# Scores in four quadrants of TensorE and two PSUM banks, in one visit with the preceding pair's values

## The chip, the core and the metric

The kernel runs on one core of a Trainium2 chip. The metric is the device time of one execution in microseconds (us); the number given for a kernel is the median of several executions. A profiled execution leaves a trace with the start and length of each instruction. Its engines are named PE (TensorE's matmuls), PEld (TensorE's loads of weights), DVE (VectorE), ACT (ScalarE), POOL (GpSimd) and SP (SyncE, which issues the DMAs here).

## The reference

A chunked local attention is followed by two feed-forward layers:

```python
# q, k, v: (4, 8, 768, 64); mem_k, mem_v: (4, 8, 8, 64)
for c in range(24):                       # chunks of 32 queries
    k_full = concat(mem_k, k[c*32-16 : c*32+32+8])   # cut at the ends of the sequence
    scores = q_c @ k_full.T / 8
    a = exp(scores - max); a = a / (sum(a) + 1e-9)
    out_c = a @ v_full
x = out as (3072 tokens, 512)
h = x @ w_in;  g = max(0.01*h, h);              y = g @ w_out     # d_ff 2048
h = y @ w_in2; g = h * clip(h + 3, 0, 6) / 6;   result = g @ w_out2
```

## The kernel before

**Attention.** A "pair" is 64 tokens, two chunks of 32, with all eight heads, taken as HP = 4 pairs of heads; the 4 x 768 tokens make 48 pairs. A pair's context has W = 96 columns: 64 tokens, 16 left, 8 right, 8 of memory; a table of masks takes out what a chunk must not see. The steps of a pair are one function each: `load_qk` and `load_v` (SP), `a_scores` (PE, L317: eight float32 matmuls of 64x64x96, the two heads of a pair of heads on the tiles (0,0) and (64,64) of the array, all into one PSUM bank), `a_masked` (DVE, L327: scale, mask and copy to SBUF), `a_most` (DVE, L339: maximum), `a_exp` (ACT, L346, four activations that also sum), `a_sums` (DVE, L357, L358), `a_norm` (POOL, L362), the transposition of the weights, `a_values` (PE, L394: eight float32 matmuls, 96 rows by 64 columns, on the tiles (0,0) and (0,64)), and `a_xh` (ACT, L406) with `a_xl` (DVE, L412), which split the result into a high and a low part for the feed-forward matmuls. The transposition is made by PE and ACT for the first 16 pairs (`a_turn_pe` L380, `a_turned` L385), by 12 DVE stream transposes a pair after that (`a_turn` L372).

**Feed-forward.** Each layer goes over six blocks of TB = 512 tokens, each block over NF = 16 steps of 128 hidden columns. A step has 24 matmuls of 128x128x512 (`mm3`, L458; three products of high and low parts, high*high, high*low and low*high, stand for one of higher precision): 12 for the hidden columns into a bank `ph`, then, a step later, 12 for the four output parts into the four banks `py0` to `py3`, in which a block's 16 steps are summed. So a block has 384 of them. Between the two, ACT and DVE apply the activation and split (`act_1` to `act_4`: L477, L491, L500, whose result `gl` the last matmuls read). At a block's end `done` copies the four banks, `py0` and `py2` by DVE (L532), `py1` and `py3` by ACT (L534), and `stored` (L543) sends them out. Weights come as 64-bit numbers and are turned into a high and a low part by ACT and DVE (`w_upper` to `w_low`, L217 to L257), during block 0 for layer 1 of the model (called layer 0 in the code) and during block 5 for the other.

**Order.** All steps are put into one `Program` with an engine, an assumed time (the table `TIME`), a due time, the steps they come after, and the buffers they take and free (`rings`: PSUM has four banks `py`, two `ph`, two `pa`). `Program.order` then lists them: each engine always takes the ready step that is due first and for whose buffers there is room, and the code is emitted in that order. Pairs 0 to 7 run in a prologue (TensorE has `keep_warm` matmuls, L551, as long as it has nothing else before the assumed time BEGIN = 30), pairs 8b to 8b + 7 among the feed-forward matmuls of block b - 1. A pair's scores and its values are two steps with due times 7 apart (times `spread`), each in a `pa` bank of its own, so each interrupts the feed-forward matmuls by itself. The prologue's scores and values use the `py` banks.

Of the kernel before, what the change touches and what calls it, by code (L numbers as in the profile page):

```python
# [23 lines left out]
    scores=0.9, masked=0.56, most=0.55, exp=1.65, sums=0.36, norm=0.83, turn=0.6, turned=0.57, turn4=0.95,  # L24
    values=0.6, xh=0.4, xl=0.45, half=1.36, act=0.58, six=0.69, gh=0.6, gl=0.69, done=0.66, warm=0.22,
# [10 lines left out]
class Program:  # L36
# [15 lines left out]
    def order(self, filler):  # L52
# [81 lines left out]
def tile_kernel(  # L134
# [34 lines left out]
    P = 128  # L169
# [23 lines left out]
    masks = at.tile([P, 3, W], F32, tag="masks", name="masks")  # L193
# [6 lines left out]
    rings = dict(w=NF, raw=NRAW, wa=2, ye=4, aT=2, gh=2, gl=2, x=2, py=4, ph=2, pa=2, qk=NBUF, v=NBUF, yn=1, oo=NRAW)  # L200
# [81 lines left out]
    e_t, s_t, m_t, aT_t, px_t, x_t, in_t = {}, {}, {}, {}, {}, {}, {}  # L282
# [24 lines left out]
    def pa(pr, name, early="py"):  # L307
        tag = early if pr < NPB else "pa"
        return ps.tile([P, 512], F32, tag=tag, name=name, bufs=4 if tag == "py" else 2)

    def a_scores(pr):
        qt, kt, _ = inputs(pr)
        pt = pa(pr, f"psc{pr}")
# [7 lines left out]
        e_t[pr] = pt  # L321

    def a_masked(pr):
        p, pt = pr % PPB, e_t[pr]
        mv = 1 if p == 0 else 2 if p == PPB - 1 else 0
        e = sb.tile([P, HP, W], F32, tag="ye", name=f"e{pr}", bufs=4)
        nc.vector.scalar_tensor_tensor(  # L327
            out=e,
            in0=pt[:, :HP * W].rearrange("p (h w) -> p h w", h=HP),
            scalar=SCALE,  # L330
            in1=masks[:, mv:mv + 1, :].to_broadcast([P, HP, W]),
            op0=ALU.mult,
            op1=ALU.add,
        )
        e_t[pr] = e
# [40 lines left out]
    def a_turn_pe(pr):  # L376
        e = e_t.pop(pr)
        pt = pa(pr, f"pt{pr}", "pa")
        for hp in range(HP):
            nc.tensor.transpose(pt[:W, hp * P:(hp + 1) * P], e[:, hp, :], ident)  # L380
        aT_t[pr] = pt

    def a_turned(pr):
        t = at.tile([W, HP, P], F32, tag="aT", name=f"aT{pr}", bufs=2)
        nc.scalar.copy(out=t.rearrange("p h c -> p (h c)"), in_=aT_t[pr][:W, :])  # L385
        aT_t[pr] = t

    def a_values(pr):
        t, vt = aT_t.pop(pr), inputs(pr)[2]
        pt = pa(pr, f"px{pr}")  # L390
# [7 lines left out]
        px_t[pr] = pt[:, :HP * PT].rearrange("p (h c) -> p h c", h=HP)  # L398
# [15 lines left out]
    x_ready, values_done = {}, []  # L414

    def attention(pr, t, turned_by_pe, spread):
# [11 lines left out]
        vl = add("SP", 0.45, due(-1), load_v, pr, takes=vv if blk else (), after=[] if blk else [a], nbytes=W * 2048)  # L428
        s, e, x = [(tag, ("s", pr))], [("ye", ("e", pr))], [("x", (0, blk))]
        before = [values_done[x] for x in [pr - (3 if blk == 0 else 2)] if x >= 0]  # L430
        c = add("PE", T["scores"], due(0), a_scores, pr, after=[a] + before, takes=s, frees=qk if blk else ())
# [14 lines left out]
        p = [(tag, ("v", pr))]  # L446
        c = add("PE", T["values"], due(7.0), a_values, pr, after=[c, vl], takes=p, frees=aT + vv)
        values_done.append(c)
        first = pr % NPB == 0
        c = add("ACT", T["xh"], due(7.8), a_xh, pr, after=[c] + ([] if first else x_ready[blk][:1]),  # L450
                takes=x if first else ())
        d = add("DVE", T["xl"], due(8.3), a_xl, pr, after=[c], frees=p)
        x_ready.setdefault(blk, []).extend([c, d] if first else [d])
# [53 lines left out]
    def output(layer, blk, f, part):  # L507
# [3 lines left out]
        if f == 0 and part == 0:  # L511
            acc[layer, blk] = [
                ps.tile([P, 512], F32, tag="py", name=f"py{layer}_{blk}_{c}", bufs=4) for c in range(4)
            ]
        dst = acc[layer, blk]
# [29 lines left out]
    def keep_warm():  # L545

        if "warm" not in late:
            late["warm"] = ps.tile([P, TB], F32, tag="ph", name="warm", bufs=2)
        for c in range(2):
            r = slice(c * 256, c * 256 + 256)  # L550
            nc.tensor.matmul(late["warm"][:, r], idle[:, :P], idle, start=True, stop=True)  # L551
# [22 lines left out]
    def start():  # L574
# [3 lines left out]
        for e in range(2):  # L578
# [4 lines left out]
            nc.vector.memset(masks[r0, 1, 0:LC], NEG)  # L583
            nc.vector.memset(masks[r1, 2, CTX - RC:CTX], NEG)
# [13 lines left out]
    for pr in range(NP):  # L598
# [3 lines left out]
        else:  # L602
            every = NF * length[0, blk - 1] / NPB
            spread = 1.6 if blk == 1 else 1.5
# [125 lines left out]
```

## Time and profile before

| | us |
|---|---|
| median of 3 runs | 1170.42 |
| lowest and highest | 1169.61, 1171.92 |
| the profiled execution | 1171.43 |
| its span, first to last instruction | 1169.7 |
| PE, DVE, ACT, POOL busy | 1160.6, 601.4, 471.2, 40.5 |
| prologue, before the first feed-forward matmul | 35.23 |
| blocks 0 / 1 to 3, each / 4 / 5 of the first layer | 112.71 / 102.20 / 101.15 / 87.04 |

TensorE's granted clock is 1.00 of full speed in all slices of the page. A matmul's start is exact, its end is modelled, and neighbours overlap: the step from one start to the next is what it costs. A float32 matmul on a part of the array leaves two records ("x16" for eight matmuls).

### The profile page before, as it was taken

What the parts mean: (1) busy time and instruction counts of PE and PEld (TensorE: products, weight loads), DVE (VectorE), ACT (ScalarE), POOL (GpSimd) and SP (SyncE); (2) the same over time, 40 slices, a digit from 0 to 9 for tenths busy, and PEclk for the clock granted to TensorE, in tenths of its full rate; (3) what the DMA queues carried; (4) which work ended last, traced back from release to release, by engine and by line L of the source; (5) the groups of instructions that cost most, each with busy time, mean ns of one, the idle gap of its engine ahead of it and who ended that gap; (6) DMA issues with size and microseconds to landing.
All of it is one profiled execution on the core that took longest, in us unless ns stands there. A gap on an engine that the chain in (4) does not pass through costs nothing.

```text
span 1169.7 us, 16189 instructions
## 1 busy us (share of the span) xinstructions
PE 1160.6 (99%) x6338; PEld 936.1 (80%) x6338; DVE 601.4 (51%) x1291; ACT 471.2 (40%) x1073; POOL 40.5 (3%) x54
## 2 busy tenths in 40 slices
PE   9999999999999999999999999999999999999998
PEld 7777777777777777777888888888888888888886
DVE  5999975555555556554698943323223223222222
ACT  6878842333334333332677633223223223222222
POOL 1100000000000000000000000000000000000000
PEclk9999999999999999999999999999999999999999
DMA  8455521121112112111553500100100100000000
GB/s 240 157 186 181 184 94 37 42 85 37 37 47 81 37 43 84 37 37 35 171 163 126 185 32 4 69 1 13 60 1 22 51 1 5 33 1 14 24 1 36
DMA packets 38572, 78.64 MB, mean 67 GB/s; under 512 B 4192, under 2 KB 16480, under 8 KB 38496
## 3 DMA queue, kind: packets, MB, share of 16 engines
q1 hardware_dynamic: 38496, 77.61, 20.9%
q8 instruction: 50, 0.82, 0.3%
q14 instruction: 26, 0.21, 0.1%
HBM read 65.01 MB, written 12.58 MB: 66 GB/s over the span
## 4 chain that ended last, share of the span: by engine, by line
PE 91%; DVE 5%; DMA 2%; issue 1%; ACT 1%; SPq 0%; DVEq 0%; ACTq 0%
PE py L458 42%; PE ph L458 42%; PE psc L317 3%; PE px L394 2%; DMA raw<-in_moe_w_out_dram 2%; PE warm L551 1%; DVE w L257 1%; DVE wa L238 1%; DVE raw L245 1%; DVE wa L227 1%; DVE wa L231 1%; PE pt L380 0%; DVE gl L500 0%; ACT wa L217 0%; DVE e L327 0%
## 5 line engine op out<-in xcount | busy, mean ns | idle before, releaser
L458 PE MATMUL ph<-xh,w 128*128 128x512 f32 x768 | 259.2, 398 | 1.8 <-ACT w L251 1.0
L458 PE MATMUL ph<-yh,w 128*128 128x512 f32 x768 | 252.0, 389 | 0.0
L458 PE MATMUL py<-gh,w 128*128 128x512 f32 x768 | 243.3, 396 | 0.9 <-DVE w L257 0.5
L458 PE MATMUL py<-w,gh 128*128 128x512 f32 x768 | 236.4, 389 | 0.0
L486 DVE SCALAR_TENSOR_TENSOR ph<-g,ph 128x512 f32<-128x512 f32 x96 | 66.8, 696 | 281.5 <-ACT g L480 281.4
L480 ACT ACTIVATE g<-ph,three 128x512 f32<-128x512 f32 x96 | 66.3, 690 | 294.5 <-PE ph L458 294.5
L458 PEld LDWEIGHTS ph<-xh,w 128*128 128x128 f32 x768 | 143.3, 188 | 38.3 <-DVE w L257 4.0
L458 PEld LDWEIGHTS ph<-yh,w 128*128 128x128 f32 x768 | 144.2, 188 | 30.0
L458 PEld LDWEIGHTS py<-gh,w 128*128 128x128 f32 x768 | 141.0, 188 | 33.9 <-DVE w L257 3.8
L458 PEld LDWEIGHTS py<-w,gh 128*128 128x128 f32 x768 | 144.2, 188 | 29.9
L458 PE MATMUL ph<-xl,w 128*128 128x512 f32 x384 | 149.8, 390 | 0.4 <-DVE xl L412 0.4
L458 PE MATMUL py<-gl,w 128*128 128x512 f32 x384 | 150.0, 390 | 0.0
L458 PE MATMUL py<-w,gl 128*128 128x512 f32 x384 | 149.4, 389 | 0.0
L458 PE MATMUL ph<-yl,w 128*128 128x512 f32 x384 | 149.4, 389 | 0.0
L477 ACT ACTIVATE ph<-ph 128x512 f32<-128x512 f32 x96 | 55.9, 582 | 161.9 <-PE ph L458 161.8
L372 DVE STREAM_TRANSPOSE aT<-e 32x128 f32<-32x128 f32 x384 | 115.7, 301 | 8.4 <-POOL e L362 3.1
L346 ACT ACTIVATE e<-e,mx 128x96 f32<-128x96 f32 x192 | 69.6, 365 | 100.3 <-DVE mx L339 95.8
L500 DVE TENSOR_TENSOR gl<-ph,gh 128x512 fp32r<-128x512 f32 x96 | 66.2, 690 | 73.1 <-ACT gh L491 72.8
L502 DVE SCALAR_TENSOR_TENSOR gl<-ph,gh 128x512 fp32r<-128x512 f32 x96 | 66.3, 691 | 55.6 <-ACT gh L493 55.6
L458 PEld LDWEIGHTS py<-gl,w 128*128 128x128 f32 x384 | 72.1, 188 | 15.0
L458 PEld LDWEIGHTS py<-w,gl 128*128 128x128 f32 x384 | 72.0, 188 | 15.0
L458 PEld LDWEIGHTS ph<-yl,w 128*128 128x128 f32 x384 | 72.0, 188 | 14.9
(52 smaller groups left out, 942.6 us busy)
## 6 DMA issues: line engine op xcount, KB each, us to landing
raw<-in_moe_w_in_dram SPq DMA_DIRECT2D x32, 512.0 KB, 3.6
raw<-in_moe_w_out_dram SPq DMA_DIRECT2D x32, 512.0 KB, 3.6
k<-in_k_dram SPq DMA_DIRECT2D x40, 192.0 KB, 2.6
v<-in_v_dram SPq DMA_DIRECT2D x40, 192.0 KB, 2.5
y_dram<-yo SPq DMA_DIRECT2D x24, 256.0 KB, 2.5
yn<-y_dram SPq DMA_DIRECT2D x6, 1024.0 KB, 5.2
out_dram<-oo SPq DMA_DIRECT2D x24, 256.0 KB, 2.1
q<-in_q_dram SPq DMA_DIRECT2D x40, 128.0 KB, 2.0
```

The costliest lines, as they stand in the source:

```text
L227: nc.vector.tensor_scalar(out=a, in0=a, scalar1=LEAST, scalar2=MOST, op0=ALU.max, op1=ALU.min)
L231: nc.vector.tensor_scalar(out=a, in0=a, scalar1=3, scalar2=0x3FFFFFF8, op0=ALU.logical_shift_left, op1=ALU.bitwise_and)
L317: nc.tensor.matmul(pt[e * PT:(e + 1) * PT, hp * W:(hp + 1) * W], qt[r, hp, :], kt[r, hp, :], start=True, stop=True, tile_position=(e * D, ...
L346: nc.scalar.activation(out=e[:, hp, :], in_=e[:, hp, :], func=AF.Exp, bias=mx[:, hp:hp + 1], accum_out=su[:, hp:hp + 1],)
L372: nc.vector.transpose(out=t[c, :, r], in_=e[r, :, c])
L394: nc.tensor.matmul(pt[e * D:(e + 1) * D, hp * PT:(hp + 1) * PT], vt[:, c], t[:, hp, e * PT:(e + 1) * PT], start=True, stop=True, tile_posi ...
L458: nc.tensor.matmul(dst, a, b, start=first and i == 0, stop=last and i == len(terms) - 1)
L477: nc.scalar.activation(out=ph, in_=ph, func=AF.Prelu, alpha=0.01)
L480: nc.scalar.activation(out=g, in_=ph, func=AF.Relu, bias=three, scale=1.0)
L486: nc.vector.scalar_tensor_tensor(out=ph, in0=g, scalar=6.0, in1=ph, op0=ALU.min, op1=ALU.mult)
L500: nc.vector.tensor_sub(out=gl, in0=ph, in1=gh.bitcast(F32))
L502: nc.vector.scalar_tensor_tensor(out=gl, in0=ph, scalar=1.0 / 6.0, in1=gh.bitcast(F32), op0=ALU.mult, op1=ALU.subtract)
```

## The change

From pair 8 on, a pair's scores and the values of the pair before are one step on PE, a "visit" (`visit`, `visit_step`), and share one PSUM tile of two banks: scores of head pairs 0 and 1 in columns 0 to 191 of bank 0, those of 2 and 3 in the same columns of bank 1, and the values in columns 192 to 447 of bank 1. There is one such tile (`pa`, one buffer of two banks in place of two of one bank). The eight score matmuls go over all four 64x64 quadrants of the array: head pairs of bank 0 on the diagonal as before, those of bank 1 on (0,64) and (64,0), so that in the order written four in a row are on four quadrants. For the latter the two heads of a pair of heads stand in exchanged partitions, which `a_values` undoes by the columns it reads. The first pairs' scores go to `py`, their values to `ph`, their transposes to the one `pa` tile. The four output banks become two tiles of two banks, `py0` with parts 0 and 1, `py1` with 2 and 3. The mask table keeps the common mask alone; the sequence's first and last pair get two small DVE memsets each. `keep_warm` runs until the last PE transposition of the prologue is evacuated. Due times and assumed times change with it.

```diff
-    scores=0.9, masked=0.56, most=0.55, exp=1.65, sums=0.36, norm=0.83, turn=0.6, turned=0.57, turn4=0.95,
-    values=0.6, xh=0.4, xl=0.45, half=1.36, act=0.58, six=0.69, gh=0.6, gl=0.69, done=0.66, warm=0.22,
+    visit=1.2, scores=0.75, masked=0.56, most=0.55, exp=1.65, sums=0.36, norm=0.83, turn=0.6, turned=0.57, turn4=0.95,
+    values=0.85, xh=0.4, xl=0.45, half=1.36, act=0.58, six=0.69, gh=0.6, gl=0.69, done=0.66, warm=0.22,
...
-                    if e == "PE" and filler and now < filler[2]:
+                    if e == "PE" and end[filler[2]] is None:
...
-    rings = dict(w=NF, raw=NRAW, wa=2, ye=4, aT=2, gh=2, gl=2, x=2, py=4, ph=2, pa=2, qk=NBUF, v=NBUF, yn=1, oo=NRAW)
+    rings = dict(w=NF, raw=NRAW, wa=2, ye=4, aT=2, gh=2, gl=2, x=2, py=2, ph=2, pa=1, pt=1, qk=NBUF, v=NBUF, yn=1, oo=NRAW)
...
     def a_scores(pr):
...
-        for hp in range(HP):
-            for e in range(2):
-                r = slice(e * D, (e + 1) * D)
-                nc.tensor.matmul(
-                    pt[e * PT:(e + 1) * PT, hp * W:(hp + 1) * W], qt[r, hp, :], kt[r, hp, :],
-                    start=True, stop=True, tile_position=(e * D, e * PT),
-                )
+        for m in range(HP // 2):
+            for j in range(2):
+                hp = j * HP // 2 + m
+                for e in range(2):
+                    r, n = slice(e * D, (e + 1) * D), e ^ j
+                    nc.tensor.matmul(
+                        pt[n * PT:(n + 1) * PT, j, m * W:(m + 1) * W], qt[r, hp, :], kt[r, hp, :],
+                        start=True, stop=True, tile_position=(e * D, n * PT),
+                    )
...
     def a_masked(pr):
...
+        for n in range(2):
+            if p == 0:
+                nc.vector.memset(e[n * PT:n * PT + CH, :, 0:LC], NEG)
+            if p == PPB - 1:
+                nc.vector.memset(e[n * PT + CH:(n + 1) * PT, :, CTX - RC:CTX], NEG)
...
     def a_values(pr):
...
-                c = slice(hp * P + e * D, hp * P + (e + 1) * D)
+                c, n = slice(hp * P + e * D, hp * P + (e + 1) * D), e ^ 2 * hp // HP
...
-                    pt[e * D:(e + 1) * D, hp * PT:(hp + 1) * PT], vt[:, c], t[:, hp, e * PT:(e + 1) * PT],
+                    pt[e * D:(e + 1) * D, hp * PT:(hp + 1) * PT], vt[:, c], t[:, hp, n * PT:(n + 1) * PT],
...
+    def visit(pr):
+        if pr < NP:
+            a_scores(pr)
+            pt = p_t[pr]
+        else:
+            pt = pa(f"px{pr}")
+        if pr > NPB:
+            a_values(pr - 1, pt[:, 1, HP // 2 * W:HP // 2 * W + HP * PT])
...
-        c = add("PE", T["scores"], due(0), a_scores, pr, after=[a] + before, takes=s, frees=qk if blk else ())
+        if blk == 0:
+            before = [values_done[x] for x in [pr - 3] if x >= 0]
+            c = add("PE", T["scores"], due(0), a_scores, pr, after=[a] + before, takes=s)
+        else:
+            c = visit_step(pr, t, [a], s, qk)
...
-        c = add("PE", T["values"], due(7.0), a_values, pr, after=[c, vl], takes=p, frees=aT + vv)
+        if blk == 0:
+            p = [("ph", ("v", pr))]
+            c = add("PE", T["values"], due(7.0), a_values_first, pr, after=[c, vl], takes=p, frees=aT + vv)
+            values_done.append(c)
+            finish(pr, c, due(7.0), p)
+        else:
+            pending[:] = [c, vl, aT + vv]
+    def visit_step(pr, t, after=(), takes=(), frees=()):
+        if not pending:
+            return add("PE", T["scores"], t, visit, pr, after=after, takes=takes, frees=frees)
+        p = [*takes] or [("pa", ("s", pr))]
+        c = add("PE", T["visit"], t, visit, pr, after=[*pending[:2], *after], takes=p,
+                frees=pending[2] + [*frees])
+        finish(pr - 1, c, t, p)
+        return c
...
-                ps.tile([P, 512], F32, tag="py", name=f"py{layer}_{blk}_{c}", bufs=4) for c in range(4)
+                ps.tile([P, 2, 512], F32, tag="py", name=f"py{layer}_{blk}_{c}", bufs=2) for c in range(2)
...
-            spread = 1.6 if blk == 1 else 1.5
-            attention(pr, block_at[0, blk] - 9.5 * spread - every * (NPB - 1 - i), blk == 1, spread)
+            attention(pr, block_at[0, blk] - 3.5 - every * (NPB - i), blk == 1, 1.3)
+    visit_step(NP, block_at[0, NB - 1] - 3.5)
```

`finish` adds `a_xh` and `a_xl` of a pair behind the step that made its values, as `attention` did before.

How the rows of an engine move, at three places. First PE at steps 12 to 14 of block 1, before: the values of one pair (`px`, L394) stand between output matmuls, the next pair's scores (`psc`, L317) six matmuls later.

```order
L458 MATMUL py_1_1_1903<-gh_1_12_2491,w_12_1462 128x512 x2
L458 MATMUL py_1_1_1903<-gl_1_12_2499,w_12_1462 128x512
L394 MATMUL px_2536<-aT_2501,v_75 64x64 [waits DMAHW3_49,DVE_49,PE_49]
L394 MATMUL px_2536<-aT_2501,v_75 64x64 [waits DVE_49]
L394 MATMUL px_2536<-aT_2501,v_75 64x64 x6
L458 MATMUL py_1_2_1904<-gh_1_12_2491,w_12_1462 128x512 x2
L458 MATMUL py_1_2_1904<-gl_1_12_2499,w_12_1462 128x512
L458 MATMUL py_1_3_1905<-gh_1_12_2491,w_12_1462 128x512 x2
L458 MATMUL py_1_3_1905<-gl_1_12_2499,w_12_1462 128x512
L317 MATMUL psc_2556<-k_74,q_72 64x96 [waits DMAHW5_49,DMAHW4_49,PE_49]
L317 MATMUL psc_2556<-k_74,q_72 64x96 x7
L458 MATMUL ph_1_14_2565<-xh_768,w_14_1610 128x512
```

After, at the same steps (L329 scores, L410 values):

```order
L512 MATMUL ph_1_13_2497<-xl_742,w_13_1530 128x512
L512 MATMUL ph_1_13_2497<-xh_741,w_13_1530 128x512
L329 MATMUL psc_2515<-k_74,q_72 64x96 [waits DMAHW5_49,DMAHW4_49,PE_49]
L329 MATMUL psc_2515<-k_74,q_72 64x96 x7
L410 MATMUL psc_2515<-aT_2479,v_75 64x64 [waits DMAHW3_49,DVE_49]
L410 MATMUL psc_2515<-aT_2479,v_75 64x64 [waits DVE_49]
L410 MATMUL psc_2515<-aT_2479,v_75 64x64 x6
L512 MATMUL py_1_0_1883<-gh_1_12_2483,w_12_1468 128x512 [waits Activation_49]
L512 MATMUL py_1_0_1883<-gh_1_12_2483,w_12_1468 128x512
```

Scores and values now follow one another with no feed-forward matmul between, into the same tile, at the end of the hidden matmuls. Such a visit stands 31 times in blocks 1 to 4, each 48 feed-forward matmuls behind the one before; a last one has values alone. In block 0 there are eight merged visits, and the PE transposes stand by themselves some 30 feed-forward matmuls behind each; before, block 0 had seven visits of scores, six of them followed directly by transposes of the pair before, and eight of values.

Second DVE at the same place, before:

```order
L500 TENSOR_TENSOR gl_1_13_2545<-ph_1_13_2505,gh_1_13_2534 128x512 [waits PE_49,Activation_49]
L412 TENSOR_TENSOR xl_1914<-px_2536,xh_1913 128x4x64 [waits Activation_49]
L327 SCALAR_TENSOR_TENSOR e_2572<-psc_2556,masks 128x384 [waits PE_49]
L339 TENSOR_REDUCE mx_2576<-e_2572 128x4 [waits DVE_49]
L357 TENSOR_SCALAR su_2578<-su_2578 128x4 [waits Activation_49]
L358 RECIPROCAL su_2578<-su_2578 128x4 [waits DVE_49]
L500 TENSOR_TENSOR gl_1_14_2607<-ph_1_14_2565,gh_1_14_2599 128x512 [waits Activation_49]
```

After:

```order
L338 SCALAR_TENSOR_TENSOR e_2541<-psc_2515,masks 128x384 [waits PE_49]
L351 MEMSET e_2541 32x4x8 [waits DVE_49]
L351 MEMSET e_2541 32x4x8
L431 TENSOR_TENSOR xl_1892<-psc_2515,xh_1891 128x4x64 [waits Activation_49]
L554 TENSOR_TENSOR gl_1_13_2550<-ph_1_13_2497,gh_1_13_2533 128x512
L356 TENSOR_REDUCE mx_2558<-e_2541 128x4 [waits DVE_49]
L374 TENSOR_SCALAR su_2560<-su_2560 128x4 [waits Activation_49]
```

The maximum came directly behind the masked scores; now the low part `xl` of the pair before (which waits for ACT) and a feed-forward `gl` stand between them, and in this pair two memsets.

Third ACT at the end of the program, before:

```order
L480 ACTIVATE g_5_15_9372<-ph_5_15_9353,three 128x512 [waits PE_49]
L493 ACTIVATE gh_5_15_9381<-ph_5_15_9353 128x512 [waits DVE_49]
L534 COPY oo_1_9399<-py_5_1_8925 128x512 [waits DMAHW0_49,PE_49]
L534 COPY oo_3_9406<-py_5_3_8927 128x512 [waits DMAHW4_49,DMAHW2_49,DMAHW7_49,DVE_49,PE_49]
L725 UNCONDITIONAL_BRANCH
```

After:

```order
L534 ACTIVATE g_5_15_9325<-ph_5_15_9306,three 128x512 [waits PE_49]
L547 ACTIVATE gh_5_15_9334<-ph_5_15_9306 128x512 [waits DVE_49]
L589 COPY oo_1_9352<-py_5_0_8879 128x512 [waits DMAHW0_49,DVE_49]
L589 COPY oo_3_9359<-py_5_1_8880 128x512 [waits DMAHW4_49,DMAHW7_49,DMAHW2_49,DVE_49]
L777 UNCONDITIONAL_BRANCH
```

ACT's copies of parts 1 and 3 (`oo_1`, `oo_3`) waited for PE; now they wait for DVE, whose copies of parts 0 and 2 read the same tiles.

## Rows read from the trace of the kernel before

**Rows 1.** The page: busy time and share of each engine.

```profile
PE 1160.6 (99%) x6338; PEld 936.1 (80%) x6338; DVE 601.4 (51%) x1291; ACT 471.2 (40%) x1073; POOL 40.5 (3%) x54
```

**Rows 2.** Busy by stretch (blocks 0, 1, 4, 5): us, engines, PEclk, DMA, GB/s.

```profile
core 0: us, PE busy (x) PEld busy (x) DVE busy (x) ACT busy (x) POOL busy (x), PEclk, DMA share, GB/s
...
35.23:147.94 112.71, 109.24 (x658) 81.71 (x657) 106.13 (x213) 91.58 (x213) 6.64 (x8) 1.00 0.59 184
147.94:250.14 102.20, 102.20 (x641) 80.71 (x640) 60.15 (x161) 36.20 (x109) 6.62 (x8) 1.00 0.18 53
...
454.54:555.69 101.15, 101.15 (x626) 80.10 (x624) 54.46 (x152) 33.52 (x99) 6.62 (x8) 1.00 0.16 48
555.69:642.73 87.04, 87.04 (x386) 72.07 (x385) 71.30 (x127) 61.34 (x106) 0.00 (x0) 1.00 0.47 154
```

**Rows 3.** Timeline, PE, scores in block 1: start, length, engine, operation.

```profile
182.27 0.40 PE L458 MATMUL py<-gl,w 128*128 128x512 f32 x1
...
182.60 0.88 PE L317 MATMUL psc<-k,q 64*64 64x96 f32 x16
183.40 0.50 PE L458 MATMUL ph<-xh,w 128*128 128x512 f32 x1
...
183.74 0.39 PE L458 MATMUL ph<-xl,w 128*128 128x512 f32 x1
```

**Rows 4.** Timeline, PE, values among feed-forward matmuls in block 0.

```profile
45.81 0.39 PE L458 MATMUL ph<-xh,w 128*128 128x512 f32 x1
46.12 0.69 PE L394 MATMUL px<-aT,v 96*64 96x64 f32 x16
46.74 0.50 PE L458 MATMUL ph<-xh,w 128*128 128x512 f32 x1
47.08 0.39 PE L458 MATMUL ph<-xl,w 128*128 128x512 f32 x1
```

**Rows 5.** Timeline, PE, the prologue's end: scores, values, scores.

```profile
33.01 0.88 PE L317 MATMUL psc<-k,q 64*64 64x96 f32 x16
33.81 0.69 PE L394 MATMUL px<-aT,in 96*64 96x64 f32 x16
34.43 0.88 PE L317 MATMUL psc<-k,q 64*64 64x96 f32 x16
```

**Rows 6.** Timeline, PE: window 182.55 to 182.61; four transposes in block 0.

```profile
182.60 0.30 PE L317 MATMUL psc<-k,q 64*64 64x96 f32 x2
...
52.15 0.64 PE L380 MATMUL pt<-ident,e 128*96 128x128 f32 x4 [0.23 <-POOL e L362]
52.55 0.47 PE L458 MATMUL ph<-xh,w 128*128 128x512 f32 x1
```

**Rows 7.** Timeline, DVE, POOL, PE, ACT: one pair behind its scores, block 1.

```profile
183.52 0.56 DVE L327 SCALAR_TENSOR_TENSOR e<-psc,masks 128x384 f32<-128x384 f32 x1 [1.57 <-PE psc L317]
...
184.12 0.55 DVE L339 TENSOR_REDUCE mx<-e 128x4 f32<-128x384 f32 x1
...
186.89 0.83 POOL L362 TENSOR_TENSOR e<-e,su 128x384 f32<-128x384 f32 x1 [11.90 <-DVE su L358]
...
188.32 3.78 DVE L372 STREAM_TRANSPOSE aT<-e 32x128 f32<-32x128 f32 x12
...
193.16 0.69 PE L394 MATMUL px<-aT,v 96*64 96x64 f32 x16
...
193.90 0.37 ACT L406 CAST xh<-px 128x256 fp32r<-128x256 f32 x1 [0.78 <-PE px L394]
```

**Rows 8.** Waits in block 0: for what, total us, times, longest.

```profile
PEld ph L458 <- DVE w L257: 4.0, 10, 0.7
PEld py L458 <- DVE w L257: 3.8, 7, 0.9
```

**Rows 9.** Timeline, the last copies and the last matmul.

```profile
1164.50 0.69 DVE L532 COPY oo<-py 128x512 f32<-128x512 f32 x1 [0.67 <-PE py L458]
...
1164.75 0.39 PE L458 MATMUL py<-w,gl 128*128 128x512 f32 x1
1166.07 0.59 ACT L534 COPY oo<-py 128x512 f32<-128x512 f32 x1 [1.66 <-DMA out_dram<-oo]
```

More of the change, by code (lines that the diff above doesn't have):

```diff
@@ L192, in tile_kernel @@
     ident = at.tile([P, P], F32, tag="ident", name="ident")
-    masks = at.tile([P, 3, W], F32, tag="masks", name="masks")
+    masks = at.tile([P, HP // 2, W], F32, tag="masks", name="masks")
     idle = at.tile([P, 256], BF, tag="idle", name="idle")
@@ L412, in a_xl, with finish @@
         nc.vector.tensor_sub(out=xl[:, :, c], in0=px_t.pop(pr), in1=xh[:, :, c].bitcast(F32))
-    x_ready, values_done = {}, []
+    x_ready, values_done, pending, opened = {}, [], [], []
+    def finish(pr, c, t, p):
+        blk = pr // NPB
+        first = pr % NPB == 0
+        c = add("ACT", T["xh"], t + 0.8, a_xh, pr, after=[c] + ([] if first else x_ready[blk][:1]),
+                takes=[("x", (0, blk))] if first else ())
+        d = add("DVE", T["xl"], t + 1.3, a_xl, pr, after=[c], frees=p)
+        x_ready.setdefault(blk, []).extend([c, d] if first else [d])
+    def visit(pr):
[6 more added lines that the diff above has]
+            a_values(pr - 1, pt[:, 1, HP // 2 * W:HP // 2 * W + HP * PT])
     def attention(pr, t, turned_by_pe, spread):
@@ L445, in attention @@
                         frees=e if i == 3 else ())
-        p = [(tag, ("v", pr))]
-        c = add("PE", T["values"], due(7.0), a_values, pr, after=[c, vl], takes=p, frees=aT + vv)
[L448 to L453, printed above, removed]
+        if blk == 0:
+            p = [("ph", ("v", pr))]
+            c = add("PE", T["values"], due(7.0), a_values_first, pr, after=[c, vl], takes=p, frees=aT + vv)
+            values_done.append(c)
+            finish(pr, c, due(7.0), p)
+        else:
+            pending[:] = [c, vl, aT + vv]
[7 more added lines that the diff above has]
+        return c
     def mm3(dst, terms, first, last):
@@ L511, in output @@
         if f == 0 and part == 0:
-            acc[layer, blk] = [
-                ps.tile([P, 512], F32, tag="py", name=f"py{layer}_{blk}_{c}", bufs=4) for c in range(4)
+            pairs = [
+                ps.tile([P, 2, 512], F32, tag="py", name=f"py{layer}_{blk}_{c}", bufs=2) for c in range(2)
             ]
+            acc[layer, blk] = [pairs[c // 2][:, c % 2, :] for c in range(4)]
         dst = acc[layer, blk]
@@ L545, in keep_warm @@
     def keep_warm():
-        if "warm" not in late:
-            late["warm"] = ps.tile([P, TB], F32, tag="ph", name="warm", bufs=2)
+        t = pa("opening", True)
         for c in range(2):
             r = slice(c * 256, c * 256 + 256)
-            nc.tensor.matmul(late["warm"][:, r], idle[:, :P], idle, start=True, stop=True)
+            nc.tensor.matmul(t[:, 1, r], idle[:, :P], idle, start=True, stop=True)
     def load_y(blk):
@@ L616, in add_output @@
         layer, blk, f = key
-        p = [("py", (layer, blk, c)) for c in range(4)]
+        p = [("py", (layer, blk, c)) for c in range(2)]
         free = [("gh", key), ("gl", key)] + ([("w", (layer, f))] if blk == NB - 1 else [])
@@ L627, in add_output @@
                 e = add(eng, T["done"], t + length * (0.3 + 0.07 * c), done, layer, blk, c,
-                        after=[a if c < 2 else b] + (swapped if layer else []), takes=take, frees=[p[c]])
+                        after=[a if c < 2 else b] + (swapped if layer else []), takes=take, frees=[p[c // 2]])
                 evicted[layer, blk, c] = add("SP", 0.4, t + length * (0.5 + 0.07 * c), stored, layer, blk, c,
@@ L664, in tile_kernel @@
     with tc.manual_schedule():
-        for _, _, fn, args in program.order((keep_warm, T["warm"], BEGIN)):
+        for _, _, fn, args in program.order((keep_warm, T["warm"], opened[-1])):
             fn(*args)
```

55 lines of the change are left out of this document (31 added, 24 removed).

## The prediction

> **What bounds the kernel now.** I read the page's busy table first: TensorE is busy 1160.6 of 1169.7 us, the next engine, VectorE, half of that [rows 1]. A saving must therefore come out of TensorE's own stream. The table by stretch says from which part [rows 2]. Block 5 runs the 384 feed-forward matmuls and no attention in 87.04 us, a pace of 87.04 / 384 = 0.2267 us. Block 1 runs the same 384 matmuls and eight pairs in 102.20 us, blocks 2 and 3 last as long, and block 4 takes 101.15. TensorE is never idle in any of these and has the full granted clock. So attention costs 3 x 15.16 + 14.11 = 59.6 us there, about 1.9 a pair. Block 0 differs: 112.71 us, TensorE idle for 3.5 of it, VectorE busy for 106.13, that is 94%. It has two limits at once.
>
> The timeline of TensorE shows what a pair costs. A visit for scores [rows 3]: the first score starts 0.33 behind the last feed-forward matmul, the next feed-forward matmul 0.80 after that, and the one after it 0.34 later, where 0.227 is the pace. Two ordinary gaps are in it, so the visit costs 0.33 + 0.80 + 0.34 - 0.45 = 1.02 us. A visit for values costs 0.31 + 0.62 + 0.34 - 0.45 = 0.82 [rows 4]. With 31 and 32 of them in blocks 1 to 4 this makes 31 x 1.02 + 32 x 0.82 = 57.9, close to the 59.6 of the table. These two prices are what the change is about.
>
> **One visit in place of two.** Blocks 1 to 4 will have 31 merged visits and one with values alone. The kernel before has merged work once, at the end of the prologue: scores, values, scores back to back, 0.80 from scores to values and 0.62 from values to scores [rows 5]. These are the same lengths as alone, so the change of tile shape is inside them, and merging saves one way in and one way out. A merged visit with scores as slow as today costs 0.33 + 0.80 + 0.62 + 0.34 - 0.45 = 1.64, 0.20 less than the 1.84 of two.
>
> **Four quadrants.** A matmul of scores leaves two records, 16 in all for eight matmuls. They start two at a time: the first starts at 182.60, and the stretch up to 182.61 holds two already [rows 6]. Eight such steps fill about 0.66 of the 0.80, 0.08 each. Four transposes with 128 columns over the whole array take 0.40, 0.10 each [rows 6], 0.075 for 96 columns. So a step takes as long as one record's columns need, and two tiles run side by side in it. Before, these two are on the diagonal. The change gives four consecutive matmuls all four quadrants, the two that share columns going to different banks. Tiles above one another are shown by no row. The bounds are nothing saved, and half of the eight steps, 4 x 0.08 = 0.32. I take 0.32: the diagonal tiles [rows 3] and the values' tiles beside one another [rows 4] already overlap fully, so neither a shared set of rows nor a neighbouring set of columns has held a tile back. A merged visit is then 1.64 - 0.32 = 1.32, and blocks 1 to 4 cost 31 x 1.32 + 0.82 = 41.7 in place of 57.9: **-16.1 us**.
>
> **The chain behind a visit.** One tile of two banks now holds a pair's scores and the values of the pair before, so the next visit waits for this pair's whole chain. The chain of one pair can be read from its rows [rows 7]: masked scores start 0.12 behind the last score and take 0.56, the maximum ends at 184.67, POOL divides from 186.89 to 187.72, and the transposes of 3.78 us end at 192.10; that is 8.7 from the visit's end at 183.40. In the new order VectorE's queue has xl of the preceding pair and a gl between masked scores and maximum. Xl waits for ScalarE's xh, which waits for masked scores, since both read the tile. Xh takes 0.37 [rows 7], xl estimated as much, gl some 0.7 as VectorE's other passes over 512 columns (the copy in [rows 9]), 0.1 for a wait: 1.6 us more, so the transposed weights are ready 10.3 behind the visit. Two steps last 48 x 0.2267 = 10.9, and the next values come a way out, a way in and the scores' 0.48 later, at 11.6. So about 1.3 us are left and I cost the chain at nothing. If it grows beyond that cover, the whole excess is TensorE's, 31 times. Feed-forward evacuations queued behind xl on VectorE have a whole step, over 5 us, to spare. The two small memsets for edge pairs lie on VectorE, which is 54 to 59% busy in these blocks [rows 2], and cost nothing.
>
> **Block 0.** By its visits alone: 7 x 1.02 + 8 x 0.82 = 13.7 before, 8 x 1.32 = 10.6 after, -3.1. But six of its transposes followed a scores visit directly and now go into the stream by themselves, with a way in and out of their own (0.1 to 0.2 each), and VectorE is nearly full. The loads of weights wait for VectorE's conversions already, 4.0 and 3.8 us [rows 8]: time that TensorE gives up here is mostly spent waiting for them. On the other side VectorE's queue has new waits in it there (xl for xh), worth up to +2, eight of some 0.25. Bounds -3.1 and +2; I take **-1.0**, a third of the gain, nearer to the row with VectorE's 94%.
>
> **Prologue.** Scores of pair 9, 0.80 us [rows 5], leave it for the first merged visit, already counted in block 0. Warm-up matmuls run until the last transposition of pair 7 is evacuated instead of for a fixed time, and scores take two banks. Bounds -2 and +1.5; taken **-0.5**.
>
> **Tail and evacuation.** Columns 0 and 1 of the output share a tile, 2 and 3 too, so the VectorE copy waits for both columns' matmuls and ScalarE's copy waits for VectorE's. At the end copy 2 began at 1164.50, before the last matmul at 1164.75; copy 3 waited until 1166.07 for a transfer [rows 9], that of copy 0, whose buffer it takes. Copy 0 now starts three matmuls later, 3 x 0.227 = 0.7, and the transfer with it. Bounds 0 and +0.7; taken **+0.6**. Between blocks 24 hidden matmuls, 5.4 us, cover the same waits. Layer 1 is otherwise untouched.
>
> **Sum.** On the profiled execution's own 1171.4 us (its span 1169.7): -16.1 - 1.0 - 0.5 + 0.6 = -17.0, 1154.4. The median of the runs, 1170.4, is 1.0 lower than that execution, so I predict a median of **1153.4**.
>
> **Rival 1: the quadrants bring nothing.** Scores keep eight steps, only merging pays: 31 x 0.20 = 6.2; with -0.6 in block 0, -0.5 and +0.6 the median is 1170.4 - 6.7 = 1163.7. The mechanism: each matmul is two passes over one tile; if starts are strictly in program order, a second pass waiting for its first holds back the next tile's, and one matmul a step is the most, however many tiles. Eight steps for eight matmuls is just what that gives, for today's scores as well. Against it stands that the first two records start together [rows 6], within 0.01 us, where that mechanism has the first pass alone. The Trainium skill, "TensorE: Matmul & The Clock Gate", section "Part 3: Packing small matmuls — row/col tiling", says that matmuls start and end strictly in order; by that rule and two passes the time would be this rival's 1163.7, and the trace agrees with it only if the two records that start together are the passes of one matmul. The Trainium skill, "TensorEngine Tiling (Array Packing)", section "Gotcha 1: PSUM Pressure", says that different row tiles cannot access one bank at the same time; by that the change's (0,0) and (64,64), both in bank 0, would take turns and the time again be this rival's, but the scores of today, diagonal in one bank, start together in the trace, which disagrees. A part of the gain is possible too: if starts need as much time as in the values' steps (0.62 for eight pairs of starts, less the change of shape, 0.06 each), eight pairs take 0.48 in place of 0.33, 0.15 x 31 = 4.6 later, 1158.
>
> **Rival 2: slower, the chain does not fit.** In blocks 1 to 4 the next visit waits for the transposes. It starts to cost beyond 1.3 us over my 10.3, and from 1.3 + 0.52 (what a pair saves, 1.84 - 1.32) = 1.8 over, the kernel is slower than before. With 2.0 over, 0.7 x 31 = 21.7, so 1175. For it: every step of the chain is in order on VectorE, and in the rows above gl also waits for ScalarE. Against: VectorE and ScalarE are 54 to 59% and 33 to 35% busy in these blocks [rows 2], and POOL does nothing else. The Trainium skill, "TensorEngine Tiling (Array Packing)", section "PSUM Bottleneck", warns that a faster TensorE can leave the evacuation as the limit; no run here shows it yet.
>
> **How the numbers follow.** Forecast 0.70, its own range 1148.5 to 1159 (block 0 at -3.1 and prologue at -2 are 3.6 less, 1149.8; half of one way in or out less at each of 31 merged visits, 0.04 each, another -1.3; both at their upper ends are +5, 1158.4). Rival 1 with its partial form beyond that 0.20. Rival 2: 0.06, of which 0.05 slower. Smaller stalls of the chain, still faster, 0.04. A measurement of this kernel can tell about 0.2% from no change, so faster 0.93, same 0.02, slower 0.05. The range takes in rival 1 and a microsecond beyond: 1148.5 to 1165.
>
> **What would show it.** Right: in blocks 1 to 4 1.77 us from the start of the last feed-forward matmul before a visit to that of the second behind it, four score records starting together, 98.0 us for each of blocks 1 to 3 (102.20 - 8 x 0.52), TensorE never idle there, block 0 near 111.7, layer 1 at 87.04 a block. Rival 1: score records still two at a time, blocks at 100.6. Rival 2: waits of the first values matmul for VectorE's transposes, blocks over 102. I am wrong altogether if blocks 1 to 3 are not shorter by 1 us at least, or if block 0 gives back more than 3.

## The result and the profile after

The changed kernel takes 1161.08 us (1160.1 to 1161.63), the kernel before 1170.26 beside it: a ratio of 0.9913, interval 0.9899 to 0.9927. That is 9.2 us less, where 17.0 were forecast. The time lies in the range, nearer to rival 1's 1163.7 than to the likeliest 1153.4. The profile shows that rival 1 is nevertheless not what happened. The profiled execution took 1160.1 us, 1.0 less than the median, and the one before, 1171.43, 1.2 more than its own: so the two profiles lie 11.3 apart, where the medians lie 9.2 apart.

The page of the changed kernel, busy time and share of each engine:

```profile
PE 1140.4 (98%) x6350; PEld 926.1 (80%) x6350; DVE 601.8 (52%) x1303; ACT 473.3 (41%) x1073; POOL 42.7 (4%) x54
```

TensorE is busy 20.2 us less than in [rows 1], and the span is 11.4 shorter: it stands idle 8.8 us more. Where, the table by stretch tells (prologue, blocks 0 to 5; columns as in [rows 2]):

```profile
0.00:41.06 41.06, 33.87 (x447) 25.61 (x447) 22.79 (x63) 25.29 (x91) 7.31 (x14) 1.00 0.63 188
41.06:153.01 111.95, 106.29 (x672) 81.15 (x673) 107.78 (x216) 92.37 (x211) 9.31 (x9) 1.00 0.59 182
153.01:250.83 97.82, 97.82 (x642) 78.82 (x640) 59.85 (x166) 36.14 (x108) 7.00 (x9) 1.00 0.18 57
250.83:348.64 97.81, 97.81 (x641) 78.82 (x640) 54.93 (x154) 35.21 (x106) 6.61 (x9) 1.00 0.18 55
348.64:446.45 97.81, 97.81 (x641) 78.82 (x640) 55.30 (x158) 35.22 (x106) 6.62 (x9) 1.00 0.18 55
446.45:543.76 97.31, 97.31 (x625) 78.45 (x624) 53.73 (x152) 33.58 (x98) 5.84 (x8) 1.00 0.16 52
543.76:630.80 87.04, 87.04 (x385) 72.10 (x384) 72.15 (x129) 61.77 (x106) 0.00 (x0) 1.00 0.45 152
```

Beside the kernel before, stretch by stretch (us; the last row is what lies behind the start of the last matmul, 1164.75 of 1169.7 before, 1152.83 of 1158.3 now):

| stretch | before | after | difference | forecast |
|---|---|---|---|---|
| prologue | 35.23 | 41.06 | +5.8 | -0.5 |
| block 0 | 112.71 | 111.95 | -0.8 | -1.0 |
| blocks 1 to 4 | 407.75 | 390.75 | -17.0 | -16.1 |
| block 5 and the second layer | 609.06 | 609.07 | 0.0 | 0 |
| end | 4.95 | 5.47 | +0.5 | +0.6 |
| sum | 1169.7 | 1158.3 | -11.4 | -17.0 |

One stretch is off: the prologue, 6.3 us longer than forecast. That is a little more than the 5.6 us by which the sum is off. (One trace gives a prologue to a microsecond or so: the kernels e3 and e4 below leave it as it is, and in their traces it ends at 39.86 and 40.08.)

The visits look as forecast. TensorE's timeline in block 1, a merged visit, and a window of the first 0.03 us of it:

```profile
182.68 0.39 PE L512 MATMUL ph<-xh,w 128*128 128x512 f32 x1
183.00 0.56 PE L329 MATMUL psc<-k,q 64*64 64x96 f32 x16
183.49 0.69 PE L410 MATMUL psc<-aT,v 96*64 96x64 f32 x16
184.11 0.72 PE L512 MATMUL py<-gh,w 128*128 128x512 f32 x2
...
183.00 0.31 PE L329 MATMUL psc<-k,q 64*64 64x96 f32 x4
```

From scores to values it is 0.49 in place of the 0.80 of [rows 5], 0.31 less (forecast 0.32). The window up to 183.03 holds four records, where [rows 6] had two (and has no third up to 182.70). The first two matmuls, on (0,0) and (64,64), are the same before and after. If the two records of [rows 6] were the passes of the first matmul alone, the second would hold the others back now as it did then; but four start. So the four are four tiles: four quadrants run at once, with scores of both row halves in one bank too.

The prologue, PE and ACT: the first pair's transposes, warm-ups, the copy of the transposes, warm-ups, values.

```profile
12.46 0.64 PE L397 MATMUL opening<-ident,e 128*96 128x128 f32 x4 [0.19 <-POOL e L379]
...
12.94 0.82 PE L605 MATMUL opening<-idle 128*128 128x256 bf16 x6
...
13.79 0.58 ACT L402 COPY aT<-opening 96x512 f32<-96x512 f32 x1 [0.32 <-PE opening L605]
...
14.42 0.81 PE L605 MATMUL opening<-idle 128*128 128x256 bf16 x6 [0.67 <-ACT aT L402]
...
15.17 0.69 PE L410 MATMUL px<-aT,in 96*64 96x64 f32 x16
```

Transposes and warm-ups write one and the same tile, `opening`. The copy needs the transposes alone, which end at about 12.94, but it starts behind the six warm-ups of L605 that were issued after them, at 13.79. Then the next six warm-ups wait 0.67 us for the copy, and the values, which stand behind those in TensorE's queue, for them. The waits of the prologue (for what, total us, times, longest) say that this repeats:

```profile
ACT aT L402 <- PE opening L605: 5.9, 8, 1.0
PE opening L605 <- ACT aT L402: 5.0, 7, 0.7
```

These two kinds of wait were not in the prologue before.

### The profile page after: what moved, and what is told of

It reads as the page before. It is cut to its first block, busy times and chain, and to the rows that moved or that the text cites. A ratio compares the mean times of both kernels' runs of the same rounds, so it can differ in the third digit from the quotient of the medians.

```text
span 1158.3 us, 16198 instructions
## 1 busy us (share of the span) xinstructions
PE 1140.4 (98%) x6350; PEld 926.1 (80%) x6350; DVE 601.8 (52%) x1303; ACT 473.3 (41%) x1073; POOL 42.7 (4%) x54
## 4 chain that ended last, share of the span: by engine, by line
PE 93%; DVE 4%; DMA 1%; ACT 1%; issue 1%; POOL 0%; ACTq 0%; DVEq 0%; POOLq 0%
PE py L512 44%; PE ph L512 43%; PE psc L410 2%; PE psc L329 2%; PE opening L605 1%; DMA raw<-in_moe_w_out_dram 1%; DVE wa L238 1%; DVE w L257 1%; DVE raw L245 1%; DVE wa L231 0%; PE px L410 0%; DVE e L338 0%; ACT aT L402 0%; PE opening L397 0%; DVE wa L227 0%
## 5 line engine op out<-in xcount | busy, mean ns | idle before, releaser
L512 PE MATMUL ph<-xh,w 128*128 128x512 f32 x768 | 252.5, 390 | 0.4 <-ACT xh L425 0.3
L512 PEld LDWEIGHTS ph<-xl,w 128*128 128x128 f32 x384 | 72.1, 188 | 15.3 <-DVE xl L431 0.3
```

Source lines behind the costliest of these rows:

```text
L512: nc.tensor.matmul(dst, a, b, start=first and i == 0, stop=last and i == len(terms) - 1)
```

## The experiments

**e1: a tile of its own for the warm-ups.** Theory A: this sharing of a tile is what made the prologue longer. Theory B, its rival: the pairs now run in series through one transpose buffer and score tiles of two banks. The edit gives warm-ups and transposes one bank each, as two tiles, in place of two banks of one tile; the order of TensorE's instructions in the prologue is unchanged.

```diff
+    po = open_scope.enter_context(tc.tile_pool(name="po", bufs=1, space=bass.MemoryType.PSUM))
...
-        t = ps.tile([P, 2, 512], F32, tag="pa", name=name, bufs=1)
...
+            if opening not in late:
+                late[opening] = po.tile([P, 1, 512], F32, tag=opening, name=opening, bufs=1)
...
-        t = pa("opening", True)
+        t = pa("warm", "warm")
...
-            nc.tensor.matmul(t[:, 1, r], idle[:, :P], idle, start=True, stop=True)
+            nc.tensor.matmul(t[:, 0, r], idle[:, :P], idle, start=True, stop=True)
```

> The changed kernel with one edit: the prologue's warm-up matmuls write a one-bank PSUM tile of their own instead of the second bank of the tile that takes the transposes; order and everything else as in the changed kernel. Theory A (the prologue got longer, 35.2 to 41.1 us, because warm-ups and the copies of the transposes wait for each other through the shared tile; ScalarE's copies waited 5.9 us for warm-ups and warm-ups 5.0 us for copies): the prologue ends at 35.5 to 37, the median is 1155 to 1157. Theory B (one transpose buffer in place of two and score tiles of two banks put the pairs in series): the prologue still ends near 41, the median stays at 1161.

Measured: 1157.25 us, ratio 0.9881 (0.9865 to 0.9897), against 0.9913 of the changed kernel: 3.8 us less. Its prologue ends at 37.86. Theory A holds for the larger part, but 2.6 us to the old 35.23 are left; prologue and median both lie a little above what theory A gave (37 and 1157). What the rest is, the waits of its prologue show, and its timelines of ACT (18 to 24 us) and PE:

```profile
PE px L414 <- ACT aT L406: 2.6, 2, 2.1
ACT wa L219 <- DMA raw<-in_moe_w_in_dram: 2.2, 1, 2.2
```

```profile
17.95 0.58 ACT L406 COPY aT<-opening 96x512 f32<-96x512 f32 x1
20.76 0.69 ACT L219 ACTIVATE wa<-raw 128x512 f32<-128x512 f32 x1 [2.23 <-DMA raw<-in_moe_w_in_dram]
...
23.57 0.61 ACT L406 COPY aT<-opening 96x512 f32<-96x512 f32 x1
...
24.23 0.69 PE L414 MATMUL px<-aT,in 96*64 96x64 f32 x16 [2.08 <-ACT aT L406]
```

ScalarE's first conversion of weights (L219) stands ahead of the fourth copy in its queue and waits 2.2 us for its transfer; TensorE waits 2.1 us for that copy. In the changed kernel the same conversion started at 21.10 without a wait: the prologue was late enough for the transfer. With the warm-ups out of the way, the transfer became the next limit. And behind TensorE's wait its granted clock fell to the lower level for a while, as the stretches of e1 show (the third number from the end is the granted clock as a share of 2.4 GHz), and ten warm-up records at 26 us took 2.34 us, where ten at 30 us took 1.25:

```profile
24.00:26.00 2.00, 1.69 (x35) 1.41 (x36) 1.97 (x6) 1.94 (x10) 0.83 (x1) 0.88 0.84 225
26.00:28.00 2.00, 2.00 (x11) 1.49 (x10) 1.97 (x6) 2.00 (x6) 0.83 (x1) 0.50 0.07 25
28.00:30.00 2.00, 2.00 (x37) 1.34 (x36) 0.88 (x3) 1.61 (x9) 0.00 (x0) 0.77 0.37 63
```

```profile
26.37 2.34 PE L609 MATMUL warm<-idle 128*128 128x256 bf16 x10
...
30.33 1.25 PE L609 MATMUL warm<-idle 128*128 128x256 bf16 x10
```

So most of what is left of the longer prologue is the wait for the transfer and the clock lost behind it; e8, below, takes both away.

**e5: the shared tile, in the kernel before.** The reverse test: of the change, only this sharing, with one transpose buffer in place of two, and the scores of pairs 8 to 15 behind the last copy. (Its one tile serves all transposes of the prologue in the old order, in which the second pair's are written before the first's are copied: the kernel leaves out the attention of a pair so overwritten, with the same instructions.)

```diff
         if pr < NPB:
+            return opening()[:, 0, :]
...
-            late["warm"] = ps.tile([P, TB], F32, tag="ph", name="warm", bufs=2)
+        t = opening()
...
-            nc.tensor.matmul(late["warm"][:, r], idle[:, :P], idle, start=True, stop=True)
+            nc.tensor.matmul(t[:, 1, r], idle[:, :P], idle, start=True, stop=True)
```

> The kernel before with one edit: the prologue's warm-up matmuls and its transposes share one PSUM tile of two banks, as in the changed kernel (scores of pairs 8 to 15 also come after the last copy of the prologue). Theory A (the shared tile makes warm-ups and copies wait for each other, and that is most of the longer prologue; the run with a warm-up tile of its own was 3.8 us faster than the changed kernel): the prologue ends at 38.5 to 41, the median is 1174 to 1176. Theory B (the rest of the new prologue costs it): at most 1 us more than before, 1171 to 1172.

Measured: 1176.37 beside 1170.19, ratio 1.0047 (1.0031 to 1.0064), 6.2 us more. The first block starts at 40.61 in place of 35.23, 5.4 later, and the same waits appear:

```profile
ACT aT L399 <- PE opening L566: 4.7, 6, 1.1
PE opening L566 <- ACT aT L399: 4.3, 6, 0.7
```

So the shared tile costs about what the prologue lost, without four quadrants, merged visits, new rings or a new end of the warm-ups. How much of the 5.4 us comes from the one transpose buffer, e5 does not tell; that theory B's part is small is shown by e8, below, which keeps one transpose buffer and score tiles of two banks and has a prologue of 35.71.

**e8: e1, and the first conversions of weights later.** ScalarE's conversions of the first weights come behind the fourth copy; the rest is e1.

```diff
-            b = add("ACT", T["words"], t - 4.9, w_upper, key, after=[a], takes=wa)
-            l = add("ACT", T["words"], t - 4.2, w_lower, key, after=[a])
+            late_enough = [opened[3]] if key == (0, 0, 0) else []
+            b = add("ACT", T["words"], t - 4.9, w_upper, key, after=[a] + late_enough, takes=wa)
+            l = add("ACT", T["words"], t - 4.2, w_lower, key, after=[a] + late_enough)
```

> The run with a warm-up tile of its own (prologue 37.9), and ScalarE's first two conversions of weights moved behind its fourth copy of transposes. In that run they stood ahead of it, waited 2.2 us for their transfer, and TensorE waited 2.1 us for the copy. If that wait is what is left of the longer prologue, the prologue ends at 35.5 to 36.5 and the median is 1155 to 1156 (ratio to before 0.987). If the first weights then are late for the feed-forward matmuls instead, the prologue gives back what it gains: 1157 or more.

Measured: 1155.27 us beside 1171.78, ratio 0.9869 (0.9852 to 0.9885), as expected; the fastest kernel of this study. Its stretches:

```profile
0.00:35.71 35.71, 33.07 (x454) 25.74 (x455) 22.63 (x62) 24.83 (x91) 7.57 (x14) 1.00 0.79 208
35.71:148.11 112.40, 106.22 (x672) 81.23 (x673) 107.77 (x217) 92.43 (x211) 9.55 (x9) 1.00 0.60 185
148.11:245.93 97.82, 97.82 (x642) 78.80 (x640) 59.87 (x166) 36.13 (x108) 7.04 (x9) 1.00 0.18 56
```

The prologue is 35.71, with the other gains kept, its granted clock is 1.00, and ScalarE's wait for the transfer is gone. (The intervals of e1 and e8 overlap, so that the last 2 us came from this edit rests on the traces.) The prologue is still 0.5 longer than before with one visit for scores less, no more than two traces of one prologue differ; whether something holds it (one transpose buffer, waits for POOL of 0.4) was not tried.

**e7: the old end of the warm-ups.** The planner's filler (the warm-ups, put where TensorE has no step ready) ends at the assumed time 30 again, 8 of 142 warm-ups fewer.

```diff
-                    if e == "PE" and end[filler[2]] is None:
+                    if e == "PE" and now < filler[2]:
...
-        for _, _, fn, args in program.order((keep_warm, T["warm"], opened[-1])):
+        for _, _, fn, args in program.order((keep_warm, T["warm"], BEGIN)):
```

> The changed kernel with the old end of the warm-ups (assumed time 30 in place of the last copy's end): 8 of 142 warm-up matmuls fewer, all behind the transposes of pairs 6 and 7. Each stretch of warm-ups that goes frees a copy from waiting: two of eight, at 0.7 each, so 0.7 to 1.4 us less than the changed kernel, 1159.7 to 1160.4. If the new end condition is the main cost, 4 us or more less.

Measured: 1159.94, ratio 0.9912 (0.9892 to 0.9932) against 0.9913. The new end condition is not the main cost. Whether it costs the 0.7 to 1.4 us cannot be told from these times. Its trace shows something on the other side: the prologue ends at 39.38, but in the first 10.62 us of block 0 the granted clock is 0.87 on average, where it was 1.00 in the changed kernel:

```profile
39.38:50.00 10.62, 10.60 (x71) 8.10 (x69) 9.59 (x19) 8.62 (x22) 1.09 (x1) 0.87 0.55 177
```

Block 1 then starts at 152.85, no earlier to speak of than the changed kernel's 153.01.

**e6: fewer warm-ups, with e1's tile.** None behind the copy of the first pair's transposes.

```diff
-        for _, _, fn, args in program.order((keep_warm, T["warm"], opened[-1])):
+        for _, _, fn, args in program.order((keep_warm, T["warm"], opened[0])):
```

> The run with a warm-up tile of its own, and no warm-up matmuls behind the first pair's transposition (66 in place of 142). Its prologue ended at 37.9, 2.6 later than before the change, with warm-ups on the chain of waits. If they still hold back transposes and values, as they stand ahead of them in TensorE's queue, the prologue ends at 35 to 36.5 and the median is 1154 to 1156. If the granted clock falls with less work on TensorE, the matmuls of the prologue and of block 0's beginning take longer and the median is 1158 or more. If what is left is the series of the pairs through one transpose buffer, no change, 1157.

Measured: 1160.64, ratio 0.9912 (0.9892 to 0.9933), 3.4 us more than e1 (the two intervals just touch). The table by stretch shows why (the granted clock again third from the end):

```profile
20.00:30.00 10.00, 5.02 (x73) 3.74 (x66) 7.25 (x17) 7.71 (x29) 1.65 (x2) 0.69 0.66 190
30.00:40.08 10.08, 7.91 (x93) 5.76 (x89) 7.29 (x18) 8.30 (x25) 1.65 (x2) 0.50 0.31 104
40.08:50.00 9.92, 9.92 (x54) 7.73 (x50) 8.59 (x17) 7.39 (x20) 1.09 (x1) 0.79 0.36 101
```

With TensorE half idle between 20 and 30 us (4.26 us of it waiting for the fourth copy, which here too stands behind a conversion that waits for its transfer, 2.62 us) the clock fell, was at the lower level, 1.2 GHz, from 30 to 40, and was 0.79 on average in the first 10 us of block 0, through which TensorE was busy without a gap. The warm-ups do earn their place in e1; it is the tile they write that cost. (Whether they do in e8, without that wait, was not run.) How much of the longer prologue (40.08) is the clock and how much waits of copies is not separated.

**e2: the diagonal again.** The scores of the second bank go back to the tiles (0,0) and (64,64). All else is as in the changed kernel, the shared tile too; the edit also puts the prologue's scores on the diagonal.

```diff
-                    r, n = slice(e * D, (e + 1) * D), e ^ j
+                    r, n = slice(e * D, (e + 1) * D), e
...
-                c, n = slice(hp * P + e * D, hp * P + (e + 1) * D), e ^ 2 * hp // HP
+                c, n = slice(hp * P + e * D, hp * P + (e + 1) * D), e
```

> The changed kernel with the scores of the second bank put back on the diagonal tiles (0,0) and (64,64): two quadrants, two banks, merged visits. If four quadrants at once are what shortened a visit, scores take 0.80 again in place of 0.49, a visit 1.61 in place of 1.30, blocks 1 to 3 are 2.5 us longer each (100.3), and the median is 1161 + 39 x 0.31 = 1173, above the kernel before. If merging alone gave the gain, the median stays near 1161.

Measured: 1173.35 beside 1171.37, ratio 1.0014 (1.0005 to 1.0024): without the quadrants, and with the longer prologue, the change would be no gain. A visit and a block (blocks 1 to 3 are alike):

```profile
187.26 0.88 PE L329 MATMUL psc<-k,q 64*64 64x96 f32 x16
188.06 0.69 PE L410 MATMUL psc<-aT,v 96*64 96x64 f32 x16
188.68 0.73 PE L512 MATMUL py<-gh,w 128*128 128x512 f32 x2
```

```profile
256.93:357.19 100.26, 100.26 (x641) 81.34 (x640) 54.93 (x154) 35.20 (x106) 6.61 (x9) 1.00 0.18 53
```

Scores take 0.80 again. Of the 4.39 us that a block gained (102.20 to 97.81), 100.26 - 97.81 = 2.45 are the quadrants', 0.31 a pair, and 1.94 merging's with the rest of the change, 0.24 a pair. In blocks 1 to 4 e2 is thus still faster than the kernel before; its prologue, which ends at 41.98, and block 0 take that back.

**e3 and e4: how much cover has the chain?** The maximum of a pair's scores is taken twice (e3) or four times (e4) from pair 16 on; the edit of e4:

```diff
-        nc.vector.tensor_reduce(out=mx, in_=e_t[pr], axis=AX.X, op=ALU.max, negate=True)
+        for _ in range(4 if pr >= 2 * NPB else 1):
+            nc.vector.tensor_reduce(out=mx, in_=e_t[pr], axis=AX.X, op=ALU.max, negate=True)
```

> The changed kernel with the maximum of a pair's scores taken twice from pair 16 on (VectorE, about 0.5 us more in the chain from a visit to the next). The transposes ended 1.03 us before the values in the profile of the changed kernel. If that is the slack of the chain, nothing is lost: 1161, blocks 1 to 3 at 97.8. If the chain already decides, 32 x 0.5 = 16 us more.

> The same with the maximum taken four times: about 1.5 us more in the chain. With a slack of 1.03 every visit from pair 17 on waits about 0.45 us: 32 x 0.45 = 14 us more, 1175, blocks 1 to 3 near 101.5 and the values' first matmul waiting for VectorE. If the slack is larger than it looks (other work of VectorE moves out of the way), less than 5 us.

Measured: e3 1160.7, ratio 0.9905 (0.989 to 0.9919), no loss. E4 1177.13, ratio 1.0048 (1.0031 to 1.0065): slower than the kernel before. A visit of e4 and one of its blocks:

```profile
375.74 0.56 PE L329 MATMUL psc<-k,q 64*64 64x96 f32 x16
376.23 0.33 PE L411 MATMUL psc<-aT,v 96*64 96x64 f32 x2
377.09 0.68 PE L411 MATMUL psc<-aT,v 96*64 96x64 f32 x14 [0.53 <-DVE aT L390]
```

```profile
357.52:458.94 101.42, 100.35 (x641) 80.29 (x640) 68.59 (x182) 34.37 (x108) 6.63 (x8) 1.00 0.17 53
```

In the first fence the value matmuls behind the first pair of records start 0.86 later, 0.53 of it spent waiting for VectorE's transposes. The block takes 101.42 in place of 97.81: 0.45 a pair. How long the added work is, VectorE's rows say, masked scores, maximum and transposes of one pair, first of the changed kernel and then of e4:

```profile
184.22 0.56 DVE L338 SCALAR_TENSOR_TENSOR e<-psc,masks 128x384 f32<-128x384 f32 x1 [1.37 <-PE psc L410]
...
186.16 0.54 DVE L356 TENSOR_REDUCE mx<-e 128x4 f32<-128x384 f32 x1
...
190.20 2.83 DVE L389 STREAM_TRANSPOSE aT<-e 32x128 f32<-32x128 f32 x9 [1.45 <-POOL e L379]
```

```profile
365.21 0.56 DVE L338 SCALAR_TENSOR_TENSOR e<-psc,masks 128x384 f32<-128x384 f32 x1
...
367.14 2.31 DVE L357 TENSOR_REDUCE mx<-e 128x4 f32<-128x384 f32 x4
...
372.54 2.84 DVE L390 STREAM_TRANSPOSE aT<-e 32x128 f32<-32x128 f32 x9 [1.09 <-POOL e L380]
```

Three maxima more last 2.31 - 0.54 = 1.77 us, not the 1.5 of the expectation, and the transposes start 7.33 - 5.98 = 1.35 later behind the masked scores; the other 0.4 is taken up between the sums and POOL's division (0.59 us there in the changed kernel, 0.23 in e4), which was not followed further. So the chain bears about 1.77 - 0.45 = 1.3 us more work before TensorE waits. Rival 2 is real, with its place and its price, and this kernel is on the good side of it.

## Why the prediction was right, and what in it was wrong

**What bounds, and the prices of visits: right.** Blocks 1 to 4 got 17.0 us shorter, 16.1 forecast. TensorE is busy in all of them without a gap. A merged visit is 0.32 + 0.49 + 0.62 and a way out of 0.33 less two ordinary gaps, 1.31 for the forecast's 1.32.

**Four quadrants: right.** The value taken, half of the eight steps, is what came; e2 takes exactly that away. Rival 1's mechanism (one matmul a step, since a second pass holds back the next tile's) would have let at most two records start together; four did, and e2, with the same first two matmuls, has two. The Trainium skill, "TensorEngine Tiling (Array Packing)", "Gotcha 1: PSUM Pressure", says that row tiles cannot access one bank at the same time; of the four that start together here, (0,0) and (64,64) write one bank, in different partitions, and the trace disagrees for such a pair. No run tried two row tiles on the same columns in one bank.

**The chain behind a visit: right.** A cover of 1.3 us was forecast. In block 1 of the changed kernel the last transposes and the values stand like this:

```profile
193.75 0.94 DVE L389 STREAM_TRANSPOSE aT<-e 32x128 f32<-32x128 f32 x3
...
195.72 0.69 PE L410 MATMUL psc<-aT,v 96*64 96x64 f32 x16
```

The transposes end at 194.69, 1.03 before the values; a second gl has slipped in between them (nine transposes at 190.20, three here), which the sum lacked. The weights are ready 10.58 us behind the visit's end at 184.11, where 10.3 was forecast, and that they are so near is partly luck: the second gl is 0.69 long, but the transposes start right behind POOL's division, at 190.20, where 0.60 lay between them in [rows 7]. With the slack further up the chain e4 found 1.3. A pair saves (102.20 - 97.81) / 8 = 0.55, so in these blocks the change would be a loss from 1.3 + 0.55 = 1.85 us of a longer chain, where 1.8 was forecast; e4 is a loss sooner, since it carries the prologue's 5.8 as well.

**Block 0: right in what limits it, the size uncertain.** -0.8 against -1.0. TensorE's busy time fell by 2.9 us, from 109.24 to 106.29, near the 3.1 of its visits, and 2.2 of it became waiting. VectorE is busy 107.78 of 111.95 us, and what TensorE waited for is converted weights, from ScalarE more than from VectorE; ScalarE's conversion waited for VectorE's in turn:

```profile
PE py L512 <- ACT w L251: 3.6, 6, 0.7
PE py L512 <- DVE w L257: 1.8, 6, 0.3
ACT w L251 <- DVE raw L245: 5.0, 11, 0.6
```

The 0.8 is the best of five: e1, e3, e4 and e8, whose block 0 has the same work, take 112.40 to 112.82 us for it, so that the gain there is 0.3 at most.

**The end: right**, +0.5.

**The prologue: wrong, by 6.3 us, and with it the sum.** The step that failed is "Bounds -2 and +1.5; taken **-0.5**": the measured +5.8 lies far beyond its upper bound. It counted the scores that leave the prologue and asked how long the warm-ups run, but not where they write. The diff has it in two lines:

```diff
-            late["warm"] = ps.tile([P, TB], F32, tag="ph", name="warm", bufs=2)
+        t = pa("opening", True)
```

Work that only fills TensorE's idle time then has an order with work that matters: copies wait for it, it waits for copies, and it stands ahead of values and transposes in TensorE's queue. e5 prices this at 5.4 us of prologue in the old kernel, e1 at 3.8 us of the total in the new one, where the wait for a transfer, with the clock lost behind it, takes over the rest (e8: another 2 us). That the time was in the range is luck: the forecast's own range ended at 1159, and the rest was there for rival 1, which did not occur.

With the two prologue edits the mechanism gives 1155.27 us, ratio 0.9869; the forecast 1153.4 is a ratio of 0.9855. What is left of that difference lies in the prologue (35.71, where 34.7 was forecast) and block 0 (112.40 in e8, where 111.7 was forecast), while blocks 1 to 4 saved 0.9 more than forecast.

## What to carry to other kernels

Before small matmuls are called cheap, look at how many of their records start together: if two tiles run at once in the trace, spreading consecutive matmuls over all quadrants and two banks halved their steps here and took them from 0.80 to 0.49 us, more than half of what the change saved in blocks 1 to 4. When a change moves filler work to another buffer, follow its writes as closely as those of real work: a shared tile ordered them here, though they wrote different banks of it. And when two visits become one, measure the slack of the chain that now lies between two visits (1.0 to 1.3 us here): it decides between a gain and a loss.

## What the runs showed of the hardware that was not expected

Four 64x64 float32 tiles run at once, 16 records in four groups: the same 0.08 us a step as with two. The clock, once lost, came back late: in e6, TensorE was busy without a gap from 40.08 to 50.00 and still had 0.79 on average; and a single wait of 2.1 us was followed by the lower level in e1 (0.50 from 26 to 28 us). And an earlier prologue ran into its data: e1's first transfer of weights was on its way until 20.76, and the conversion that needs it stood 2.2 us in ScalarE's queue, ahead of work that was ready.
